# Cross attention and a two-way max MLP on one core: weight pieces of two row tiles by 512 columns, and a new order of the prologue

## The chip, the core and the metric

The kernel runs on one core of a Trainium2 chip. A core has five engines with a queue of instructions each: TensorE (PE in the profile, its weight loads PEld), VectorE (DVE), ScalarE (ACT), GpSimd (POOL) and SyncE (SP), which here only issues DMA transfers. Each engine works through its own queue in order and waits on semaphores for the others. Matrix products end in eight banks of PSUM, from which ACT and DVE copy them to SBUF; POOL does not read PSUM in this kernel. The metric is the device time of one execution, in microseconds (us).

## The reference

For each of 8 batches and 8 heads, x (512 x 64) and state (32 x 64) attend to each other; the results stand side by side in the 512 channels, and an MLP with the maximum of two projections follows.

```python
scores = scale * np.matmul(x, state.transpose(0, 1, 3, 2))
a = softmax(scores)                       # over the 32 states
xread = np.matmul(a, state)
scores2 = scale * np.matmul(state, x.transpose(0, 1, 3, 2))
a2 = softmax(scores2)                     # over the 512 positions
sread = np.matmul(a2, x)
# heads side by side: (8 * 544, 512)
h1 = x @ w1                               # 512 x 1024
h2 = x @ w2
g = np.maximum(h1, h2)
return (g @ w_out).astype(np.float32)     # 1024 x 512
```

(softmax stands for the four lines that subtract the maximum, take the exponential and divide by the sum.) Inputs and output are 32-bit floats.

## The kernel before, in words

The maximum is rewritten as max(h1 - h2, 0) + h2. So the kernel needs Wd = W1 - W2 (tile `wd`, line 429), W2 times W_out (tile `wwo`, built by TensorE from the transposed W2, tile `w2t`, line 437), and W_out itself in bf16 (tile `wo`). For a batch b it multiplies the state by Wd and by W2 W_out first (`sw_mm`, line 312, tile `sw`), so that the layer-1 product of the 512 positions is the attention weights times `sw` (`l1_mm`, line 345, followed by a ReLU into `r`), and layer 2 is `r` times W_out (`l2_f`, line 363) plus the attention weights times the last part of `sw` (`l2_open`, line 358).

Around that, for each batch: x is cast to bf16 in two layouts (`cast_e`, `cast_b`), transposed (`xt_mm` on TensorE for batches 0 and 1, `xt_dma` by a transposing DMA for the others), multiplied by the transposed state `sbd` for the scores (`sc_mm`, line 225), put through the exponential (`sc_ev`, line 243, ACT), summed (`red`, line 247, DVE) and scaled (`nmul`, line 251), and the weights are transposed (`at_mm` on TensorE for batch 0, `at_dma` on SP for the others).

The prologue takes in all weights and batches 0, 1 and part of 2. Its order is written out by hand in the string `ORDER` (lines 18 to 40), which `step` (line 522) reads token by token. A token with `>V`, `>A` or `>P` is a step on DVE, ACT or POOL; one with `:n` is a step of TensorE into bank n; one with neither is a DMA issued on SP. Each engine takes its own tokens in this order.

- `ldS.0.1`, `ldS.2.8`: the state of batch 0 and of batches 2 to 7; batch 1's is issued on ACT ahead of the list.
- `ldxk.0.k`: two heads of x of batch 0 (256 KB). `ldx.b.g`: four heads (512 KB).
- `ldw1.lo.hi`, `ldw2.lo.hi`: all 512 rows of W1 or W2, columns lo to hi (512 KB, 256 columns each, so runs of 1 KB). `ldwo.f0.f1`: 256 rows of W_out (512 KB, runs of 2 KB).
- `ce.b.k`, `xt.b.k`, `sc.b.h`, `red`, `nm`, `at.b.g`: cast, transpose, scores, sums, scaling, transposed weights.
- `cw2.q`, `w2.q`: cast and transpose of the qth piece of W2. `sub.q...`: Wd of that piece. `cwo.q`: cast of a quarter of W_out.
- `ww.i.f0.f1`: row tile i of W2 W_out, summed over the column tiles f0 to f1 of W2.
- `sw.b.z`: state times a 256-column quarter z of Wd (z below 4) or times W2 W_out (z = 4). `swh.b.z`: state times a 512-column half of Wd (z = 0, 1) or times W2 W_out (z = 2).
- `l1.b.f`: column tile f of layer 1. `l2p.b.c.f0.f1`: position tile c of layer 2, summed over f0 to f1. `l2o.b.c`: its part from the attention weights. `l2.b.c`: a whole one.
- `cSm.z`: the masked cast of the state of batches 2 to 7. `std`: its transposing DMA. `atd`, `xtd`: the two others. `store`: an output.
- `idle.n.w:i`: n matmuls of zeros, w columns wide (line 444), which leave bank i with nothing of use.

Behind the list stands a loop over the batches (line 540) and an end for the last one; in it TensorE does the layers of one batch and the scores and `sw` of the next.

## Time and profile before

| | us |
|---|---|
| median of 3 runs (150.14 to 150.85) | 150.24 |
| the profiled execution | 150.17 |
| its span in the trace | 148.4 |
| TensorE matmul busy | 140.4 |
| DVE busy | 81.5 |
| ACT busy | 69.0 |
| POOL busy | 48.9 |

Times in the trace count from the span's start. In an answer by order of time the first two columns are start and duration in us, then engine, line, operation, output and inputs, how often, and in brackets the idle time ahead of it and what ended it. Rows of neighbouring instructions of one kind are merged, so their duration is the stretch from the first to the end of the last. In a row of groups, the numbers behind the first bar are the sum in us and the mean in ns. The row of a DMA issue ends with its size and the us from issue to landing. The digits of the page's rows are busy tenths in 40 equal slices of the span. A row of stretches gives the stretch, its length, the busy time of PE, PEld, DVE, ACT and POOL, the granted clock of TensorE, the DMA engines' busy share and GB/s; the granted clock is 1.00 in all of them.

### The profile page before, as it was taken

The numbers are of one execution on the slowest core, as the hardware profiler recorded it, in microseconds if no ns is written. First come the engines' busy times: TensorE is split into PE (matmuls) and PEld (weight loads), VectorE is DVE, ScalarE is ACT, GpSimd is POOL, SyncE is SP. The second block draws the span as 40 slices with busy tenths as digits, with TensorE's granted clock in tenths as the row PEclk, the third lists the DMA queues.
The fourth block names the chain that finished last, engine by engine and source line by source line (L and its number), as shares of the span: only waits on it lengthen the run. The fifth ranks groups of instructions, "written<-read, shape, count | busy, mean of one in ns | idle before, by whom it ended". The sixth has DMA issues, their size and how long they took to land. (4 is left out here: it accounts for less than half of the span.)

```text
span 148.4 us, 3137 instructions
## 1 busy us (share of the span) xinstructions
PE 140.4 (95%) x1252; PEld 70.6 (48%) x1271; DVE 81.5 (55%) x161; ACT 69.0 (47%) x132; POOL 48.9 (33%) x74
## 2 busy tenths in 40 slices
PE   6879999999999999999999999999999999999991
...
DMA  4899999974998899499599577867306032400523
GB/s 116 276 371 364 361 351 361 267 228 81 213 283 309 148 272 364 87 148 331 222 170 272 236 196 129 274 286 141 75 0 283 0 75 106 179 9 9 200 82 141
DMA packets 39283, 29.74 MB, mean 200 GB/s; under 512 B 24160, under 2 KB 36704, under 8 KB 38368
## 3 DMA queue, kind: packets, MB, share of 16 engines
...
q8 instruction: 11, 0.18, 0.5%
q10 hardware_dynamic: 272, 0.07, 0.2%
q14 instruction: 8, 0.07, 0.2%
...
## 5 line engine op out<-in xcount | busy, mean ns | idle before, releaser
L365 PE MATMUL bank<-wo,r 128*128 128x512 bf16 (+1 forms) x260 | 60.6, 372 | 0.9 <-issue 0.3
L365 PEld LDWEIGHTS <-r 128*128 128x128 bf16 x264 | 25.5, 98 | 29.2 <-issue 1.0
L94 ACT COPY h<-bank 128x512 f32<-128x512 f32 (+1 forms) x15 | 8.6, 571 | 49.7 <-PE bank L365 49.7
L350 PE MATMUL bank<-aT,sw 128*128 128x512 bf16 x127 | 29.9, 379 | 0.1
L341 DVE TENSOR_SCALAR r<-bank 128x512 bf16<-128x512 f32 x28 | 19.4, 691 | 19.1 <-PE bank L350 18.6
L252 POOL TENSOR_TENSOR a<-e,er 128x512 bf16<-128x512 bf16 x16 | 17.1, 1084 | 34.1 <-DVE er L249 20.2
L339 ACT ACTIVATE r<-bank 128x512 bf16<-128x512 f32 x36 | 21.3, 611 | 7.6 <-PE bank L350 7.2
L96 DVE CAST sw<-bank 128x512 bf16<-128x512 f32 (+1 forms) x25 | 14.8, 643 | 14.2 <-PE bank L320 14.2
L98 POOL CAST xb<-h 128x1024 bf16<-128x1024 f32 x12 | 12.1, 1040 | 23.1 <-DMA h<-in_x_dram 12.4
L350 PEld LDWEIGHTS <-sw 128*128 128x128 bf16 x128 | 12.2, 98 | 13.6 <-ACT sw L94 0.2
L96 DVE COPY h<-bank 128x512 f32<-128x512 f32 (+1 forms) x18 | 11.7, 660 | 11.0 <-PE bank L365 10.2
L98 POOL CAST xe<-h 128x512 bf16<-128x512 f32 x27 | 15.7, 622 | 4.3 <-DMA h<-in_x_dram 2.6
L360 PE MATMUL bank<-sw,aT 128*128 128x512 bf16 (+1 forms) x54 | 16.5, 372 | 0.3
L94 ACT CAST sw<-bank 128x512 bf16<-128x512 f32 (+1 forms) x27 | 13.5, 569 | 3.0 <-PE bank L320 2.9
L248 DVE TENSOR_REDUCE sums<-e 128x16 f32<-128x512 bf16 x16 | 10.6, 662 | 1.0 <-ACT e L244 1.0
L444 PE MATMUL bank<-wz 128*128 128x256 bf16 (+1 forms) x48 | 8.9, 321 | 1.2 <-DVE ones L449 1.2
L244 ACT ACTIVATE e<-bank 128x512 bf16<-128x512 f32 x16 | 8.9, 595 | 1.4 <-PE bank L236 0.9
L360 PEld LDWEIGHTS <-aT 128*128 128x128 bf16 x66 | 5.6, 98 | 5.1 <-issue 0.5
L437 PE MATMUL bank<-wo,w2t 128*128 128x512 bf16 x31 | 7.9, 380 | 0.1
L444 PEld LDWEIGHTS <-wz 128*128 128x128 bf16 x48 | 4.8, 109 | 2.6 <-DVE ones L449 1.2
L320 PE MATMUL bank<-wd,sbd 64*32 64x512 bf16 (+1 forms) x144 | 5.6, 359 | 0.3 <-DVE wd L429 0.3
L429 DVE TENSOR_TENSOR wd<-h,h 128x512 bf16<-128x512 f32 x7 | 5.8, 862 | 0.1
...
## 6 DMA issues: line engine op xcount, KB each, us to landing
...
h<-in_moe_w_dram SPq DMA_DIRECT2D x8, 512.0 KB, 9.6
h<-in_moe_w_out_dram SPq DMA_DIRECT2D x4, 512.0 KB, 9.6
h<-in_x_dram SPq DMA_DIRECT2D x4, 512.0 KB, 9.8
...
```

The source lines that it names most:

```text
L94: nc.scalar.copy(o, i)
L96: nc.vector.tensor_copy(o, i)
L98: nc.gpsimd.tensor_copy(o, i)
L244: nc.scalar.activation(out=e_view(b, hh).rearrange("p (g c) i n -> p g c (i n)", g=2), in_=p.rearrange("p (c g m) -> p g c m", c=NC, g=2), ...
L248: nc.vector.tensor_reduce(es_all[:, b, hh], e_view(b, hh), axis=AXX, op=ALU.add)
L252: (nc.gpsimd if eng == "P" else nc.vector).tensor_mul(e_view(b, hh, "a"), e_view(b, hh), d_(b)["er"][:, hh].unsqueeze(3).to_broadcast([128 ...
L339: nc.scalar.activation(out=o, in_=p, func=ACTF.Relu)
L341: nc.vector.tensor_scalar(o, p, scalar1=0.0, scalar2=None, op0=ALU.max)
L350: nc.tensor.matmul(p, SW[b][:, g, f * 128:(f + 1) * 128], AT[b][:, g].rearrange("p c t -> p (c t)"), start=(g == 0), stop=(g == 1))
L360: nc.tensor.matmul(p[:, lo:hi], AT[b][:, g, c, :], SW[b][:, g, FF + lo:FF + hi], start=(start and g == 0), stop=(stop and g == 1))
L365: nc.tensor.matmul(p[:, lo:hi], R[b][:, f, c * 128:(c + 1) * 128], wo[:, f, lo:hi], start=(start and j == 0), stop=(stop and j == len(fs) ...
L444: nc.tensor.matmul(banks[i][:, 0:w], wz[:, 0:128], wz[:, 0:w], start=True, stop=True)
```

## The change

The pieces of W1 and W2 become two row tiles (256 rows) by 512 columns, still 512 KB, now with runs of 2 KB. A piece q has the column half q // 2 and the row tiles q % 2 * 2 and the next. Its cast, transposes, eviction and differences follow: a difference is now one row tile by 512 columns (`sub.q.k`), where it was two row tiles by 256. x of batch 0 comes in two loads of four heads. The state of batch 2 is transposed by TensorE (`S.2.3`, `S2`), so that the transposing DMA has batches 3 to 7. x of batch 3 comes in two loads. Batch 0 uses `swh` for both halves of Wd where it used four `sw`. The order of the prologue is new, and with it the engine of many casts, evictions and scalings and the number of filler matmuls.

```diff
 ORDER = """
-ldS.0.1 ldxk.0.0 ldxk.0.1 ldxk.0.2 ldxk.0.3 ldw2.0.256 ldwo.0.2 ldw1.0.256 ldw2.256.512 ldwo.2.4 ldw1.256.512
-ldw2.512.768 ldwo.4.6 ldw1.512.768 ldx.1.0 ldx.1.1 ldw2.768.1024 ldwo.6.8 ldw1.768.1024 ldS.2.8 ldx.2.0 ldx.2.1
-idle.4.512:7 cS.0.1>V S.0.1:0 cS.1.2>A idle.1.256:2 S.0.1.0>V S.0.1.1>V S.1.2:1 idle.5.256:6 S.1.2.0>A S.1.2.1>A
-ce.0.0>V xt.0.0:2 idle.6.256:7 xt.0.0>A ce.0.1>A ce.0.2>A xt.0.1:6 idle.1.256:5 ce.0.3>V xt.0.1>A xt.0.2:7 xt.0.3:5
-xt.0.2>A sc.0.0:3 xt.0.3>V sc.0.0>A sc.0.1:4 idle.6.256:1 cw2.0>V sc.0.1>A red.0.0>V w2.0:0 idle.10.256:2 w2.0>A
-cwo.0>V red.0.1>V nm.0.0>P ww.1.0.2:1 ww.2.0.2:2 sub.0.2.4>V ww.3.0.2:6 ww.0.0.2:7 sub.0.0.2>V idle.4.256:4 cw2.1>A
-nm.0.1>P sw.0.0:5,3 idle.5.256:0 sw.0.0.1>V sw.0.0.0>V w2.1:4 cwo.1>V at.0.0:0 w2.1>A at.0.1:3 idle.6.256:5
-at.0.0>V at.0.1>A ww.1.2.4:1 sub.1.0.2>V ww.3.2.4:6 sub.1.2.4>V l1.0.0:5 l1.0.1:0 l1.0.0>V sw.0.1:4,3 l1.0.1>A
-ww.0.2.4:7 cw2.2>V ww.2.2.4:2 sw.0.1.1>A sw.0.1.0>A swh.1.0:5,0 w2.2:3 swh.1.0.1>A l2p.0.0.0.2:4 cwo.2>P w2.2>V
...
+ldS.0.1 ldx.0.1 ldx.0.0 ldw2.1 ldwo.0.2 ldw2.0 ldw1.0 ldw1.1 ldwo.2.4 ldx.1.1 ldw2.3 ldw2.2 ldwo.4.6 ldwo.6.8
+ldw1.2 ldw1.3 ldx.1.0 ldx.2.1 ldx.2.0 ldS.2.8 idle.4.512:7 cS.0.1>V S.0.1:6 cS.1.2>P idle.1.256:2 S.0.1.0>A
+S.0.1.1>A S.1.2:7 idle.8.256:3 S.1.2.0>A S.1.2.1>V ce.0.3>V ce.0.2>A xt.0.3:2 xt.0.2:3 xt.0.3>V idle.4.256:5
+xt.0.2>V ce.0.1>A ce.0.0>V sc.0.1:4 xt.0.1:5 sc.0.1>A xt.0.0:0 xt.0.1>V idle.6.256:6 cw2.1>A xt.0.0>V red.0.1>V
+sc.0.0:1 sc.0.0>A w2.1:6 cwo.0>P idle.10.256:2 red.0.0>V w2.1>A nm.0.1>P ww.2.0.2:7 cw2.0>A ww.3.0.2:2 nm.0.0>V
+idle.3.256:4 w2.0:3 sub.0.1>V at.0.1:4 w2.0>A at.0.0:5 idle.6.256:1 sub.0.0>V sub.1.0>V at.0.0>A ww.0.0.2:0
+ww.1.0.2:1 at.0.1>A sub.1.1>V idle.3.256:5 cwo.1>V swh.0.0:6,3 swh.1.0:5,4 swh.0.0.1>A swh.0.0.0>V ww.0.2.4:0
+swh.1.0.0>A ww.1.2.4:1 ce.1.3>V l1.0.0:3 swh.1.0.1>A ww.3.2.4:2 l1.0.0>V ce.1.2>A ww.2.2.4:7 xt.1.3:6 l1.0.1:5
+xt.1.3>A xt.1.2:4 l1.0.3:3 l1.0.1>A cw2.3>P xt.1.2>V l1.0.2:6 l1.0.3>A sc.1.1:4 l1.0.2>V l2p.0.0.0.2:5 sc.1.1>A
+cw2.2>P w2.3:3 l2p.0.0.2.4:5 red.1.1>V w2.3>A l2p.0.2.0.2:6 l2p.0.2.2.4:6 nm.1.1>V cwo.2>A w2.2:4 l2p.0.3.0.2:3
+w2.2>V l2p.0.3.2.4:3 cwo.3>P ww.3.4.6:2 ww.0.4.6:0 ww.2.4.6:7 sub.2.1>V ww.0.6.8:0 sub.2.0>V ww.3.6.8:2 ww.0>A
+ww.2.6.8:7 sub.3.1>V ww.3>A ww.1.4.6:1 ww.1.6.8:1 sub.3.0>V ww.2>A l2p.0.1.0.2:4 ww.1>A ce.1.1>V swh.0.1:0,2
+ce.1.0>P l2p.0.1.2.4:4 swh.0.1.1>A swh.0.1.0>V xt.1.1:7 xt.1.0:1 xt.1.1>V l1.0.5:2 xt.1.0>A cb.2.1>P l1.0.4:0
+l1.0.5>A l1.0.7:7 l1.0.4>V ce.2.2>P sc.1.0:1 l1.0.6:2 sc.1.0>A l1.0.7>V ce.2.1>P l2p.0.1.4.6:4 l1.0.6>A
+l2p.0.0.4.6:5 red.1.0>V cb.2.0>P swh.1.2:0,1 sw.0.4:7,2 cSm.1>A l2p.0.2.4.6:6 nm.1.0>V l2p.0.2.6.8:6 swh.1.2.0>A
+ce.2.3>P sw.0.4.1>V l2p.0.3.4.6:3 atd.1 cSm.0>A l2p.0.1.6.8:4 ce.2.0>P swh.1.1:0,2 l2p.0.0.6.8:5 sw.0.4.0>A
+swh.1.1.1>V xtd.2 std ldx.3.0 ldx.3.1 l2p.0.3.6.8:3 swh.1.2.1>A swh.1.1.0>V l2o.0.2:6 l2o.0.0:5 l2.0.2>A S.2.3:7
+l2o.0.1:4 S2>V l2.0.0>A l1.1.6:2 l2.0.1>A l1.1.4:1 l1.1.3:0 l1.1.6>A l1.1.4>V l1.1.2:6 l1.1.1:7 l1.1.3>V l1.1.2>A
+l1.1.0:5 l1.1.1>V l1.1.5:4 l1.1.0>A l1.1.7:2 l1.1.5>V sc.2.0:1 l1.1.7>A l2o.0.3:3 sc.2.1:0 sc.2.0>A l2.1.0:6
+l2.0.3>A store.0 red.2.0>V sc.2.1>A nm.2.0>P red.2.1>V l2.1.1:7 l2.1.0>V nm.2.1>P atd.2 l2.1.1>A
 """
...
-    def load_w(w, src, lo, hi):
-        h, o = lo // 512, lo // 512 * 512
-        nc.sync.dma_start(out=half(w, h)[:, :, lo - o:hi - o], in_=src[:, lo:hi].rearrange("(i p) f -> p i f", p=128))
+    def load_w(w, src, q):
+        h, i = q // 2, q % 2 * 2
+        nc.sync.dma_start(out=half(w, h)[:, i:i + 2, :],
+                          in_=src[128 * i:128 * i + 256, 512 * h:512 * h + 512].rearrange("(i p) f -> p i f", p=128))
...
-        nc.sync.dma_start_transpose(out=sbd[:, 2:B].rearrange("p b (g k) t -> p (b g) (k t)", g=2),
-                                    in_=sb[:, 2:B].rearrange("p b g z d -> p (b g z d)"))
+        nc.sync.dma_start_transpose(out=sbd[:, 3:B].rearrange("p b (g k) t -> p (b g) (k t)", g=2),
+                                    in_=sb[:, 3:B].rearrange("p b g z d -> p (b g z d)"))
...
+    def s_ev2(p, eng):
+        copy(eng, sbd[:, 2].rearrange("p k t -> p (k t)"), p[:, 0:256])
...
-        w2b[q] = stage.tile([128, 4, FQ], BF16, tag="w2b", bufs=2, name="w2b")
-        copy(eng, w2b[q], half(2, q // 2)[:, :, q % 2 * FQ:q % 2 * FQ + FQ])
+        w2b[q] = stage.tile([128, 2, 512], BF16, tag="w2b", bufs=2, name="w2b")
+        copy(eng, w2b[q], half(2, q // 2)[:, q % 2 * 2:q % 2 * 2 + 2, :])
...
-        for f in range(2):
-            for i in range(4):
-                nc.tensor.transpose(p[:, (f * 4 + i) * 128:(f * 4 + i + 1) * 128],
+        for f in range(4):
+            for i in range(2):
+                nc.tensor.transpose(p[:, (f * 2 + i) * 128:(f * 2 + i + 1) * 128],
...
-        copy(eng, w2t[:, 2 * q:2 * q + 2].rearrange("p f i t -> p (f i t)"), p)
+        h, i = q // 2 * 4, q % 2 * 2
+        copy(eng, w2t[:, h:h + 4, i:i + 2], p.rearrange("p (f i t) -> p f i t", f=4, i=2))
...
-    def w_sub(q, i0, i1, eng):
-        c = slice(q % 2 * FQ, q % 2 * FQ + FQ)
+    def w_sub(q, k, eng):
+        h, i = q // 2, q % 2 * 2 + k
         (nc.gpsimd if eng == "P" else nc.vector).tensor_sub(
-            wd[:, i0:i1, q * FQ:(q + 1) * FQ], half(1, q // 2)[:, i0:i1, c], half(2, q // 2)[:, i0:i1, c])
+            wd[:, i, h * 512:(h + 1) * 512], half(1, h)[:, i, :], half(2, h)[:, i, :])
...
         if b + 3 < B:
-            load_x(b + 3, 0, 8)
+            for g in range(2 if b == 1 else 1):
+                load_x(b + 3, g, 4 if b == 1 else 8)
```

The rest of the old order, in the same notation (the lines left out above):

```
swh.1.0.0>A l1.0.3:0 l1.0.2:5 l1.0.3>A ww.3.4.6:6 sub.2.2.4>V l1.0.2>A ww.0.4.6:7 ww.2.4.6:2 sub.2.0.2>V ww.1.4.6:1
ce.1.0>V sw.0.2:3,0 l2p.0.0.2.4:4 sw.0.2.1>A sw.0.2.0>V ce.1.1>P xt.1.0:5 l1.0.4:0 xt.1.0>V xt.1.1:3 ce.1.2>P
l1.0.4>A l1.0.5:5 xt.1.1>V ce.1.3>P xt.1.2:0 l1.0.5>A sc.1.0:3 xt.1.2>V sc.1.0>A xt.1.3:5 cw2.3>V l2p.0.0.4.6:4
xt.1.3>A l2p.0.3.0.2:0 red.1.0>V w2.3:3 sc.1.1:5 cwo.3>A w2.3>V l2p.0.3.2.4:0 nm.1.0>P l2p.0.3.4.6:0 sc.1.1>A
ww.1.6.8:1 sub.3.2.4>V ww.0.6.8:7 ww.1>A ww.2.6.8:2 sub.3.0.2>P ww.0>V l2p.0.2.0.2:3 ww.2>A l2p.0.2.2.4:3 red.1.1>V
cSm.1>A l2p.0.2.4.6:3 sw.0.3:5,1 nm.1.1>P swh.1.1:7,2 sw.0.3.1>V sw.0.3.0>A ww.3.6.8:6 cSm.0>A swh.1.1.0>V l1.0.7:5
cb.2.0>P atd.1 l1.0.6:1 swh.1.1.1>V ww.3>A l2p.0.1.0.2:7 l1.0.6>V l2p.0.1.2.4:7 cb.2.1>P l1.0.7>A l2p.0.1.4.6:7
sw.0.4:2,6 ce.2.2>P xtd.2 swh.1.2:1,5 sw.0.4.0>A l2p.0.1.6.8:7 swh.1.2.0>V ce.2.3>P l2p.0.2.6.8:3 swh.1.2.1>A
l2p.0.3.6.8:0 ce.2.0>P sw.0.4.1>A l1.1.4:2 ce.2.1>P l1.1.0:1 l1.1.4>A l1.1.3:5 l1.1.0>A l2o.0.2:3 l1.1.3>V l1.1.6:6
l1.1.1:2 l2.0.2>V l1.1.6>A l1.1.2:1 std ldx.3.0.8 l1.1.1>A l2o.0.1:7 l1.1.2>V l1.1.5:5 l1.1.7:3 l2.0.1>V l1.1.5>A
l2p.0.0.6.8:4 l1.1.7>A l2o.0.0:4 l2o.0.3:0 l2.0.0>V sc.2.0:2 sc.2.1:1 l2.0.3>V store.0 sc.2.0>A sc.2.1>A l2.1.0:6
red.2.0>V red.2.1>V nm.2.0>P nm.2.1>P l2.1.0>A l2.1.1:7 l2.1.1>A atd.2
```

17 lines of the change are left out of this document (3 added, 14 removed).

## The prediction

> **What bounds the kernel now.** I read the first page, then TensorE's order of time over the prologue, then the loads.
>
> ```profile
> span 148.4 us, 3137 instructions
> PE 140.4 (95%) x1252; PEld 70.6 (48%) x1271; DVE 81.5 (55%) x161; ACT 69.0 (47%) x132; POOL 48.9 (33%) x74
> PE   6879999999999999999999999999999999999991
> DMA  4899999974998899499599577867306032400523
> ```
>
> TensorE is busy 95% of the span, and its row drops below 9 only in the first slices and the last. But a busy TensorE at the start is partly filler: line 444 multiplies zeros to bridge waits. So I count useful work.
>
> ```profile
> 10.97 1.25 PE L444 MATMUL bank<-wz 128*128 128x256 bf16 x10
> 12.24 1.90 PE L437 MATMUL bank<-wo,w2t 128*128 128x512 bf16 x7
> 17.38 1.04 PE L437 MATMUL bank<-wo,w2t 128*128 128x512 bf16 x4
> 18.25 1.03 PE L350 MATMUL bank<-aT,sw 128*128 128x512 bf16 x3
> 48.05 0.63 PE L320 MATMUL bank<-wd,sbd 64*32 64x512 bf16 x16
> ```
>
> The first layer-1 step of batch 0 (l1.0.0, L350) starts at 18.25; the prologue's list of steps is through at 48.05, where the loop's first L320 starts. From there on nothing is edited but the size of two transfers, so I take every us by which 48.05 moves as a us at the end. The question is when l1.0.0 can start, what TensorE must do behind it, and whether it is fed.
>
> Unit prices, from differences of starts:
>
> ```profile
> 54.01 3.62 PE L350 MATMUL bank<-aT,sw 128*128 128x512 bf16 x16
> 57.46 0.63 PE L236 MATMUL bank<-sbd,xt 128*128 128x64 bf16 x16
> 15.66 0.61 PE L420 MATMUL bank<-ident,w2b 128*128 128x128 bf16 x8
> 16.11 0.61 PE L274 MATMUL bank<-ident,a 128*128 128x128 bf16 x8
> 43.18 0.63 PE L236 MATMUL bank<-sbd,xt 128*128 128x64 bf16 x16
> 43.64 0.59 PE L360 MATMUL bank<-sw,aT 128*128 128x512 bf16 x2
> 19.21 0.30 PE L320 MATMUL bank<-wd,sbd 64*32 64x256 bf16 x8
> 19.44 1.04 PE L437 MATMUL bank<-wo,w2t 128*128 128x512 bf16 x4
> 20.41 0.41 PE L320 MATMUL bank<-wd,sbd 64*32 64x512 bf16 x8
> 20.75 0.62 PE L420 MATMUL bank<-ident,w2b 128*128 128x128 bf16 x8
> ```
>
> Sixteen 512-column matmuls take 57.46 - 54.01 = 3.45, so 0.2155 each and 0.431 a pair (each l1, each two-step ww or l2p, each l2o is a pair). Eight transposes take 0.45 (16.11 - 15.66), so an xt (four) 0.225 and a w2 0.45. An sc is half of 43.64 - 43.18, 0.23. A quarter sw step: L350's four matmuls from 18.25 end at 19.11, and L437 starts at 19.44, so 0.33. A half step (swh): L437's four end at 20.30, next start 20.75, so 0.45. A quarter has 0.11 of streaming and a half 0.215, so each switch to these small tiles costs about 0.22 beside the streaming.
>
> Now the loads. They wait in one queue, and those who wait for them date the landings:
>
> ```profile
> 9.77 0.69 DVE L96 CAST w2b<-h 128x1024 bf16<-128x1024 f32 x1 [1.15 <-DMA h<-in_moe_w_dram]
> 14.13 1.04 ACT L94 CAST w2b<-h 128x1024 bf16<-128x1024 f32 x1 [1.95 <-DMA h<-in_moe_w_dram]
> 23.66 0.43 DVE L96 CAST xe<-h 128x512 bf16<-128x512 f32 x1 [0.21 <-DMA h<-in_x_dram]
> 7.09 1.55 SPq L148 DMA_DIRECT2D h<-in_moe_w_dram  x1
> h<-in_moe_w_dram SPq DMA_DIRECT2D x1, 512.0 KB, 9.9
> 28.08 1.17 SPq L141 DMA_DIRECT2D h<-in_x_dram  x1
> h<-in_x_dram SPq DMA_DIRECT2D x1, 512.0 KB, 5.6
> ```
>
> Of the 512 KB pieces behind x0, the 1st lands at 9.77, the 4th at 14.13, the 6th (issued 7.09, 9.9 to landing) at 16.99, the 10th at 23.66, the last load of all at 28.08 + 5.6 = 33.7. That is 7.22 / 5 = 1.44 a piece early and 13.89 / 9 = 1.54 over the nine.
>
> ```profile
> 2.50:3.00 0.50, 0.50 (x2) 0.00 (x0) 0.10 (x1) 0.24 (x2) 0.00 (x0) 1.00 0.57 180
> 6.00:6.50 0.50, 0.45 (x5) 0.16 (x2) 0.00 (x0) 0.50 (x2) 0.00 (x0) 1.00 0.86 184
> 8.50:9.00 0.50, 0.42 (x9) 0.41 (x10) 0.12 (x1) 0.50 (x2) 0.00 (x0) 1.00 1.06 377
> 20.00:20.50 0.50, 0.50 (x11) 0.09 (x8) 0.18 (x1) 0.45 (x2) 0.00 (x0) 1.00 1.09 350
> 28.00:28.50 0.50, 0.50 (x7) 0.26 (x4) 0.50 (x2) 0.50 (x2) 0.00 (x0) 1.00 0.87 160
> ```
>
> The last two columns are DMA share and GB/s. The queue runs full at 350 to 377 from about 8 us, but is below that in two early places: 180 at 2.5 us, while x0's four loads are issued one after the other, and 184 at 6 us, where the first 1 KB runs of W2 follow x0.
>
> **The change, part by part.** Two DMA issues fewer for x0, and the first W2 piece in 2 KB runs. Both bear on the two dips. If nothing comes of it, the first piece lands at 9.77 as before. If both dips filled to 370, 0.5 us at 180 and 0.5 us at 184 would each give back some 0.25 us, and their neighbours about as much again: 8.8. I take 9.3, the middle, since the first dip has a cause that the change removes and the second only a suspected one.
>
> Pace behind it: the early rows' 1.44 a piece mixes 1 KB runs of W with 2 KB runs of W_out. If run length is nothing, 1.44 stays; if W went at the 377 shown at 8.5 us instead of the 350 at 20 us, a piece gains 0.1. I take 0.05 for each W piece.
>
> By the Trainium skill ("DMA: Bandwidth & Descriptors", Specifications) a transfer is at line rate from runs of 512 B up, so 1 KB and 2 KB runs should go alike. By that rule the 0.05 would be nothing, 0.15 us on the sum; the windows agree so far, as 350 and 377 differ by 8% at most.
>
> The new order needs W1 and W2 in whole column halves, all four row tiles, before swh.0.0, where the old one needed a quarter for sw.0.0. So w1.1, the 5th piece, and W_out's second quarter (ldwo.2.4), the 6th, set l1.0.0. The 6th lands at 9.3 + 7.22 - 3 x 0.05 = 16.37. Then DVE, in its order, casts it (cwo.1), TensorE does ww.0.2.4 and ww.1.2.4, and l1.0.0 follows. Durations:
>
> ```profile
> L96 DVE CAST wo<-h 128x1024 bf16<-128x1024 f32 x2 | 1.3, 657 | 0.0
> 17.10 1.29 DVE L429 TENSOR_TENSOR wd<-h,h 128x512 bf16<-128x512 f32 x2
> 12.68 2.14 DVE L429 TENSOR_TENSOR wd<-h,h 128x512 bf16<-128x512 f32 x2
> 11.50 2.78 POOL L252 TENSOR_TENSOR a<-e,er 128x512 bf16<-128x512 bf16 x2 [9.05 <-DVE er L249]
> L168 ACT ACTIVATE sb<-sf,zm 128x768 bf16<-128x768 f32 x2 | 1.9, 938 | 0.0
> L94 ACT CAST sw<-bank 128x512 bf16<-128x512 f32 x23 | 12.1, 602 | 1.5 <-PE bank L320 1.5
> sf<-in_state_dram SPq DMA_DIRECT2D x1, 384.0 KB, 9.1
> aT<-a SPq DMA_TRANSPOSE x7, 3.2
> ```
>
> 16.37 + 0.66 + 0.06 + 0.86 = **17.95** for l1.0.0. The other way in is covered: w1.1 lands about 14.95, two subs (0.645 each, row at 17.10) end at 16.25, swh.0.0 with swh.1.0 beside it takes 0.45 + 0.215 = 0.67 to 16.9, before cwo.1's 17.03; its eviction on DVE behind cwo.1 ends near 17.8, under the two ww pairs.
>
> Behind l1.0.0 TensorE has the same ww, l1, l2p, l2o, l2, w2, xt and sc as before. What differs: before, five groups of small tiles are left (0.33 + 0.45 + 0.33 + 0.56 + 0.65 = 2.32: sw.0.1, swh.1.0, sw.0.2, then sw.0.3 with swh.1.1, then sw.0.4 with swh.1.2); now three (0.45 + 0.65 + 0.45 = 1.55). S.2.3, batch 2's state on TensorE, adds two transposes, 0.11. Before, l1.0.0 to 48.05 took 29.80; now 29.80 - 0.77 + 0.11 = 29.14, if it stalls as much as it did. 17.95 + 29.14 = 47.09, **0.96 earlier**. Break-even is l1.0.0 at 18.91.
>
> Fillers (41 small ones for 44) only bridge waits that the loads set; they cost nothing while the load is later, and 0.11 each if it isn't. The moves of casts and evictions between ACT, DVE and POOL lie under TensorE, with DVE and ACT about half busy, except at two places.
>
> First, S.2.8 goes to the end of the queue, and ACT holds its mask (cSm.1) ahead of swh.1.2.0, cSm.0 and sw.0.4.0. Behind them wait swh.1.1, which needs the bank that swh.1.2.0 empties, and l2o.0.2, which needs sw.0.4.0. From l1.0.0 to swh.1.1 lie 32 pairs (13.8), 4 xt (0.9), 2 sc (0.46), 2 w2 (0.9), and two groups of small tiles (1.1): 17.15, so 35.1; l2o.0.2 follows 0.45 + 0.86 later, at 36.4. ACT needs 0.94 + 0.60 + 0.94 + 0.60 + 0.1 = 3.2 from S's landing, so S may land at 33.2. When will it? x2.0 is the 16th piece: 16.37 + 10 x 1.55 - 4 x 0.05 = 31.7. S's 384 KB take 1.1 us at 350 GB/s or 2.5 at the 160 shown at 28 us, where S's short runs pass: 32.8 to 34.2. I take the middle, 33.4 to 33.5: a wait of some **0.2**.
>
> Second, batch 1's nmul moves from POOL to DVE. No row shows it on DVE. Bounds: 0.645, the sub alone, and 1.07, the sub beside POOL work (row at 12.68). From sc.1.0 at about 31.4: exponential and latency 0.8, reduction and reciprocal 0.95, nmul 0.65 to 1.07, transposing DMA 3.2: 37.0 to 37.4; l1.1.6, which needs it, comes at 37.7. No cost, with 0.3 to 0.7 to spare.
>
> The SP queue: atd.1, xtd.2 and std wait behind S's issue, as before behind x2's. xtd.2 is due at sc.2.0 near 41, atd.1 issues at about 34, xtd.2 behind it near 35.7 as in the old run, so it is hidden; std now carries five batches and is due one loop turn later. x3 in two loads adds one issue with 10 us to spare.
>
> Sum: 0.96 - 0.2 = 0.8 of the profiled run's 150.17 (span 148.4 and 1.77 around it): 149.37. The runs' median is 0.07 above the profiled one, so **149.4**.
>
> **Rivals.**
> (A) As forecast, l1.0.0 between 17.4 and 18.2: 148.6 to 149.6.
> (B) The loads come no earlier: first piece at 9.77, 6th at 16.99, l1.0.0 at 18.57, gain 0.34: 149.9. For it: the queue is full from 8 us on in both run lengths. Against: the two dips.
> (C) S too late. It passes alone at the end of the queue, in short runs behind x2. Every 0.1 us past 33.2 is 0.1 us at l2o.0.2. From 34.2 the gain is eaten; a landing at 35.0 gives 150.24 - 0.96 + 1.8 = 151.1. For it: ACT is blocked in order, and 160 GB/s at 28 us. Against: the old run, with S in the middle, had its last load in by 33.7, and the bytes are the same.
> (D) nmul on DVE beside POOL's casts. POOL has five casts of x2 just when nm.1.0 runs; in the old run the sub took 1.07 instead of 0.645 beside POOL, and POOL's multiply (two in 2.78) suffered too. If nm.1.0 waited for a whole 1.04 us cast and DVE's subs took 1.07 at swh.0.0, l1.0.0 loses 0.4 and l1.1.6 about 0.5: gain near 0, 150.2. Against: POOL is idle at the subs.
> The Trainium skill has a rule for (D) ("SBUF — State Buffer", Who interferes with whom): a DVE instruction with two SBUF inputs contends with POOL instructions that read SBUF, and the loser waits the whole instruction. The two sub rows agree; by it nm.1.0 would pay up to a full cast.
>
> **How the numbers follow.** About 0.75 us (0.5%) is what a measurement here tells from no change. A 0.45, B 0.22, C 0.21, D 0.12. Faster: A but for its last 0.1 us or so (0.43) and a little of B (0.02), 0.45. Slower: C with S landing at about 35 (0.17), and D with S's wait on top of it (0.05), 0.22. Same: the rest, 0.33, most of it B. A's own range is 148.6 to 149.6; for 8 in 10 the range goes up to 150.9, nearly to C's end.
>
> **What would show it.** Right: first w2b cast (on ACT) near 9.3 and l1.0.0 near 18.0; the loop's first L320 near 47.3; ACT idle before cSm.1 for sf near 33.4. Wrong: l1.0.0 past 18.9; TensorE idle at swh.0.1 or xt.1.0 for late loads (w1.3, x1.0); TensorE idle before L360 or the second layer-1 run. A later difference in the loop would break the premise that the end moves with 48.05.

## The result and the profile after

The changed kernel took 148.51 us (median of 6 runs, 148.14 to 148.71) against 150.19 for the kernel before (6 runs, 149.72 to 150.85): a ratio of 0.9883, with a 95% interval of 0.9857 to 0.9909. The gain is 1.68 us, a little over twice the 0.8 forecast, and the time lies 0.09 under the low end of the range. The profiled execution took 148.61.

The first page of the changed kernel, same rows as before:

```profile
span 146.8 us, 3122 instructions
PE 140.1 (95%) x1254; PEld 69.8 (48%) x1254; DVE 82.2 (56%) x160; ACT 70.5 (48%) x132; POOL 46.5 (32%) x72
PE   6599999999999999999999999999999999999991
DMA  4999999942999987995779686777406032400524
```

The span is 1.6 us shorter and TensorE's busy time 0.3: most of what went is idle time of TensorE. The order of time shows where. Line numbers are those of the changed kernel: L353 is layer 1, L323 `sw`, L441 `ww`, L433 the differences, L255 the scaling, L168 the masked cast of the state, L222 the transposes of x, L448 the filler.

```profile
9.13 1.05 ACT L93 CAST w2b<-h 128x1024 bf16<-128x1024 f32 x1
11.80 1.32 DVE L255 TENSOR_TENSOR a<-e,er 128x512 bf16<-128x512 bf16 x1
13.26 2.59 DVE L433 TENSOR_TENSOR wd<-h,h 128x512 bf16<-128x512 f32 x4
15.93 0.69 DVE L95 CAST wo<-h 128x1024 bf16<-128x1024 f32 x1
16.73 0.69 DVE L95 CAST sw<-bank 128x512 bf16<-128x512 f32 x1
17.60 0.59 PE L353 MATMUL bank<-aT,sw 128*128 128x512 bf16 x2
32.97 0.94 ACT L168 ACTIVATE sb<-sf,zm 128x768 bf16<-128x768 f32 x1 [0.28 <-DMA sf<-in_state_dram]
46.55 0.63 PE L323 MATMUL bank<-wd,sbd 64*32 64x512 bf16 x16
```

Layer 1 of batch 0 (l1.0.0) starts at 17.60 (18.25 before) and the loop at 46.55 (48.05 before). So 0.65 us come ahead of l1.0.0, and 0.85 between it and the loop, 28.95 for 29.80. From the loop's start to the span's end it is 100.25 now and 100.35 before: the 1.50 us reach the end whole.

The loads of the changed kernel, by the rows of its issues; the queue's start times come first, then what a window around single issues says (size, us to landing), for x0's two halves, W2's first piece, W_out's second quarter and the late state S (issued at 23.73):

```profile
1.26 1.00 SPq L140 DMA_DIRECT2D h<-in_x_dram  x2
2.31 0.51 SPq L147 DMA_DIRECT2D h<-in_moe_w_dram  x1
5.76 0.54 SPq L152 DMA_DIRECT2D h<-in_moe_w_out_dram  x1
```

```profile
h<-in_x_dram SPq DMA_DIRECT2D x1, 512.0 KB, 5.1
h<-in_x_dram SPq DMA_DIRECT2D x1, 512.0 KB, 6.0
h<-in_moe_w_dram SPq DMA_DIRECT2D x1, 512.0 KB, 6.8
h<-in_moe_w_out_dram SPq DMA_DIRECT2D x1, 512.0 KB, 10.2
sf<-in_state_dram SPq DMA_DIRECT2D x1, 384.0 KB, 9.2
```

The first piece lands at 2.31 + 6.8 = 9.11 and the sixth at 5.76 + 10.2 = 15.96, so (15.96 - 9.11) / 5 = 1.37 a piece where it was 1.44. And the stretches of the changed kernel (last two columns: DMA share and GB/s):

```profile
8.00:10.00 2.00, 1.84 (x30) 1.52 (x30) 1.53 (x5) 1.81 (x3) 0.00 (x0) 1.00 1.03 392
10.00:12.00 2.00, 1.88 (x24) 1.40 (x21) 1.64 (x5) 1.87 (x4) 1.48 (x2) 1.00 1.05 402
24.50:28.50 4.00, 4.00 (x20) 1.66 (x17) 2.70 (x5) 1.82 (x4) 0.95 (x1) 1.00 1.09 352
31.50:32.50 1.00, 1.00 (x8) 0.39 (x4) 0.99 (x3) 0.91 (x2) 1.00 (x3) 1.00 0.07 17
```

With runs of 2 KB the queue moves 392 to 402 GB/s; where x (runs of 1 KB) passes, 352. The last row comes back below. At the prediction's two dips the changed kernel has

```profile
2.50:3.00 0.50, 0.50 (x2) 0.00 (x0) 0.00 (x1) 0.24 (x2) 0.00 (x0) 1.00 0.57 76
6.00:6.50 0.50, 0.00 (x0) 0.00 (x0) 0.07 (x1) 0.07 (x1) 0.00 (x0) 1.00 0.99 309
```

The first dip is deeper (76 for 180 GB/s). The second is gone (309 for 184), but 209 stands at 7.5 us, where the kernel before has 350. From 2 to 8 us both kernels move the same, 274 GB/s before and 273 now. So the dips did not fill, and yet the first piece came earlier: its issue moved from 3.29 to 2.31 us, and it landed 6.8 us behind it, where it took 6.5 before.

### The profile page after: what moved, and what is told of

It reads as the page before. It is cut to its first block, busy times and chain, and to the rows that moved or that the text cites. A ratio compares the mean times of both kernels' runs of the same rounds, so it can differ in the third digit from the quotient of the medians.

```text
span 146.8 us, 3122 instructions
## 1 busy us (share of the span) xinstructions
PE 140.1 (95%) x1254; PEld 69.8 (48%) x1254; DVE 82.2 (56%) x160; ACT 70.5 (48%) x132; POOL 46.5 (32%) x72
## 5 line engine op out<-in xcount | busy, mean ns | idle before, releaser
L368 PE MATMUL bank<-wo,r 128*128 128x512 bf16 (+1 forms) x264 | 61.5, 373 | 0.1
L93 ACT COPY h<-bank 128x512 f32<-128x512 f32 (+1 forms) x18 | 10.1, 575 | 50.9 <-PE bank L368 50.0
L344 DVE TENSOR_SCALAR r<-bank 128x512 bf16<-128x512 f32 x32 | 21.9, 690 | 18.9 <-PE bank L353 17.9
L353 PE MATMUL bank<-aT,sw 128*128 128x512 bf16 x128 | 29.6, 380 | 0.0
L342 ACT ACTIVATE r<-bank 128x512 bf16<-128x512 f32 x32 | 19.4, 614 | 4.3 <-PE bank L353 4.0
L95 DVE CAST sw<-bank 128x512 bf16<-128x512 f32 x23 | 14.7, 684 | 11.8 <-PE bank L323 11.6
L255 POOL TENSOR_TENSOR a<-e,er 128x512 bf16<-128x512 bf16 x13 | 13.4, 1048 | 24.4 <-ACT e L247 14.9
L363 PE MATMUL bank<-sw,aT 128*128 128x512 bf16 (+1 forms) x66 | 19.1, 374 | 0.0
L353 PEld LDWEIGHTS <-sw 128*128 128x128 bf16 x128 | 12.0, 98 | 13.2 <-DVE sw L95 0.2
L95 DVE COPY h<-bank 128x512 f32<-128x512 f32 (+1 forms) x15 | 9.8, 660 | 10.2 <-PE bank L368 10.2
L93 ACT CAST sw<-bank 128x512 bf16<-128x512 f32 x25 | 13.2, 600 | 1.2 <-PE bank L323 1.2
L448 PE MATMUL bank<-wz 128*128 128x256 bf16 (+1 forms) x45 | 8.1, 316 | 1.2 <-DVE ones L453 1.2
L441 PE MATMUL bank<-wo,w2t 128*128 128x512 bf16 x32 | 7.8, 380 | 0.0
L239 PEld LDWEIGHTS <-xt 128*128 128x128 bf16 x128 | 5.1, 98 | 2.9 <-DVE xt L95 0.9
L433 DVE TENSOR_TENSOR wd<-h,h 128x512 bf16<-128x512 f32 x8 | 5.2, 688 | 1.3 <-DMA h<-in_moe_w_dram 1.2
L448 PEld LDWEIGHTS <-wz 128*128 128x128 bf16 x45 | 4.5, 107 | 2.7 <-DVE ones L453 1.2
```

What stands on the lines that cost most here:

```text
L93: nc.scalar.copy(o, i)
L95: nc.vector.tensor_copy(o, i)
L255: (nc.gpsimd if eng == "P" else nc.vector).tensor_mul(e_view(b, hh, "a"), e_view(b, hh), d_(b)["er"][:, hh].unsqueeze(3).to_broadcast([128 ...
L342: nc.scalar.activation(out=o, in_=p, func=ACTF.Relu)
L344: nc.vector.tensor_scalar(o, p, scalar1=0.0, scalar2=None, op0=ALU.max)
L353: nc.tensor.matmul(p, SW[b][:, g, f * 128:(f + 1) * 128], AT[b][:, g].rearrange("p c t -> p (c t)"), start=(g == 0), stop=(g == 1))
```

## The experiments

All are edits of the changed kernel unless the text says "old order". Ratios are to the kernel before, with the 95% interval.

**1. Is it the run length? w_runs_1k** loads each W piece by two transfers of 256 columns, so that runs are 1 KB again; **w_rows_1** loads it by two transfers as well, but of one row tile each, with runs of 2 KB.

In `load_w`, w_runs_1k:

```diff
+        for c in range(2):
+            nc.sync.dma_start(out=half(w, h)[:, i:i + 2, 256 * c:256 * c + 256],
+                              in_=src[128 * i:128 * i + 256, 512 * h + 256 * c:512 * h + 256 * c + 256].rearrange("(i p) f -> p i f", p=128))
```

and w_rows_1:

```diff
+        for c in range(2):
+            nc.sync.dma_start(out=half(w, h)[:, i + 1 - c, :],
+                              in_=src[128 * (i + 1 - c):128 * (i + 1 - c) + 128, 512 * h:512 * h + 512])
```

> The changed kernel, but each piece of W1 and W2 is loaded by two transfers of 256 columns (256 KB each, runs of 1 KB). Theory (the longer runs set the pace of the load queue, and the 6th piece behind x0 sets l1.0.0): the 6th piece lands at 16.4 to 17.0 instead of 15.96, l1.0.0 starts at 18.0 to 18.6 instead of 17.60, and the time is 149.0 to 149.5. Rival (run length is nothing, the gain is the order's): GB/s between 9 and 14 us as in the changed kernel (390 to 410), time 148.3 to 148.7.

> The changed kernel, but each piece of W1 and W2 is loaded by two transfers of one row tile (256 KB each, runs of 2 KB as in the changed kernel): the control for the number of transfers. Both theories: 148.2 to 148.8, l1.0.0 within 0.3 of 17.60. If more transfers cost something by themselves, it is slower here too, and what the 1 KB version loses beyond this one is the run length's.

Measured: w_runs_1k 149.35 us, 0.9928 (0.9909 to 0.9946); w_rows_1 148.42, 0.9872 (0.9851 to 0.9892). Both have twice as many transfers, and only the one with short runs loses: 0.93 us between the two, with intervals that don't meet. So the number of transfers costs nothing here, and the run length is worth some 0.8 us, about half the gain. The profile of w_runs_1k is of its longest execution (150.18), so I take the price from the medians. But the mechanism is in it: 351 GB/s from 12 to 14 us, l1.0.0 at 18.52 (theory: 18.0 to 18.6; w_rows_1 has 17.19), and behind it TensorE waits 0.50 us for x of batch 1, at 20.48.

**2. What a run costs. stream** only loads, piece behind piece, first all of W1 and W2 in 1 KB runs, then 2 KB, then 4 KB, and then x, W_out, and W1 and W2 again.

> Loads alone, nothing computed and only the first 128 rows of the output written (with zeros): in this order 4 MB of W1 and W2 in runs of 1 KB (all rows by 256 columns), 4 MB in runs of 2 KB (two row tiles by 512 columns), 4 MB in runs of 4 KB (one row tile by all columns), 4 MB of x in runs of 1 KB that follow each other in memory, 2 MB of W_out in runs of 2 KB, then 2 KB and 1 KB runs of W again. Theory (run length sets the pace of a full queue): 345 to 365 GB/s in both stretches of 1 KB runs and in x, 385 to 410 with 2 KB, at least that with 4 KB. Rival (the bank layout of W or what runs beside it sets it): no difference between 1 KB and 2 KB beyond 2%, or x unlike W.

```profile
8.00:14.00 6.00, 0.00 (x0) 0.00 (x0) 1.00 1.10 353
20.00:24.00 4.00, 0.00 (x0) 0.00 (x0) 1.00 1.05 386
26.00:32.00 6.00, 0.00 (x0) 0.00 (x0) 1.00 1.03 411
```

(Here the columns are stretch, length, DVE, POOL, granted clock, DMA share, GB/s.) In this one execution it is 353 GB/s at 1 KB, 386 at 2 KB, 411 at 4 KB: a piece of 524,288 bytes takes 1.485, 1.358 and 1.276 us. The first step saves 0.127 us for 256 runs fewer, the second 0.082 for 128 fewer: 0.50 and 0.64 ns a run over sixteen engines, so 8 to 10 ns of one engine for each run. Neither the tensor nor the place in the stream matters: x in 1 KB runs goes at 349 from 38 to 44 us, W_out in 2 KB runs at 386 to 388 from 52 to 56, and W1 and W2 later, in the reverse order, at 387 (56 to 60) and 348 to 349 (66 to 76). That leaves nothing for the rival, the layout of W. The price also dates the kernels: before, three W pieces and two of W_out between the first and sixth landing make 3 x 1.485 + 2 x 1.358 = 7.17 (7.22 in the trace); now 5 x 1.358 = 6.79 (6.85).

The Trainium skill ("DMA: Bandwidth & Descriptors", Specifications) puts line rate at 512 B and up; 353 against 386 and 411 contradict it. A section of the same page, "Why small descriptors are slow (HBM only)", names a fixed overhead per packet, which is roughly the form the three rates have.

**3. x0 in two loads: x0_four** goes back to four loads (heads 4 to 7 first, as the new order wants them); **old_x0_two** puts two loads into the old order; **x0_one** has one load of 1 MB.

```diff
-ldS.0.1 ldx.0.1 ldx.0.0 ldw2.1
+ldS.0.1 ldxk.0.2 ldxk.0.3 ldxk.0.0 ldxk.0.1 ldw2.1
...
-ldS.0.1 ldxk.0.0 ldxk.0.1 ldxk.0.2 ldxk.0.3 ldw2.0.256
+ldS.0.1 ldx.0.0 ldx.0.1 ldw2.0.256
...
-ldS.0.1 ldx.0.1 ldx.0.0 ldw2.1
+ldS.0.1 ldx.0.0.8 ldw2.1
```

> The changed kernel, with x of batch 0 in four loads of two heads (heads 4 to 7 first). Theory (the queue is what is full, so two issues more cost nothing): the first piece of W2 lands within 0.2 of 9.11, time 148.3 to 148.7. Rival (the early dips came from the four issues, as the prediction took it): the first piece lands 0.4 to 0.6 later and the time is 148.9 to 149.2.

> The kernel before, with x of batch 0 in two loads of four heads and nothing else changed. Theory (at the start the landing of the first W2 piece follows its issue, 6.2 to 7.0 us behind it in every trace so far, so two x loads less bring every piece about 1 us forward): the first piece lands near 8.8 to 9.2 instead of 9.79, l1.0.0 starts 0.6 to 1.0 earlier than 18.25, time 0.6 to 1.2 less than the kernel before. Rival (what x0_four lost belongs to the new order, which waits for heads 4 to 7 in another way): within 0.3 of the kernel before.

> The changed kernel, with x of batch 0 in one load of 1 MB. Theory (landing follows issue): W2's first piece is issued 0.5 earlier and lands near 8.6; x0 lands as a whole near 7.2 to 7.7, so its eight transposes come later but still before W2's: time 147.9 to 148.4. Rival (bytes decide, and the four heads that came first were worth something): 148.5 to 149.0.

Measured: x0_four 150.06, 0.9982 (0.9964 to 1.0000). old_x0_two 151.01, 1.0025 (0.9999 to 1.0051). x0_one 150.48, 1.0008 (0.9986 to 1.0031). From x0_four:

```profile
1.26 1.98 SPq L140 DMA_DIRECT2D h<-in_x_dram  x4
3.29 0.47 SPq L147 DMA_DIRECT2D h<-in_moe_w_dram  x1
10.32 1.04 ACT L93 CAST w2b<-h 128x1024 bf16<-128x1024 f32 x1 [1.30 <-DMA h<-in_moe_w_dram]
18.79 0.59 PE L353 MATMUL bank<-aT,sw 128*128 128x512 bf16 x2
```

Two issues more put W2's issue from 2.31 to 3.29, and its cast from 9.13 to 10.32, where ACT waits for the load. l1.0.0 is 1.19 late and most of the gain is gone. (The profiled execution takes 150.18, 1.57 over the changed kernel's: 1.23 at the loop's start, and 0.37 behind it, where the granted clock reads 0.96 from 140 us on.) So within the new order, x0's two loads carry most of it. One load is no better: x0_one issues W2's piece 0.56 earlier, at 1.75, but it lands 7.5 us later, at 9.25, and x0 as a whole at 7.36, so both its theory (an earlier piece) and its rival fell. But in the old order they bring nothing, although W2's first piece is issued at 2.30 there too:

```profile
8.93 1.03 PE L219 MATMUL bank<-ident,xe 128*128 128x128 bf16 x8
10.34 0.68 DVE L96 CAST w2b<-h 128x1024 bf16<-128x1024 f32 x1
```

The piece lands 6.9 us behind its issue, at 9.2, and is cast at 10.34: DVE works in order, and the cast stands behind the last copy of x0's transposes. It did not wait for the load (no bracket), and l1.0.0 comes at 19.52. My theory (0.6 to 1.2 us faster) fell: the load was early and its reader wasn't. Note also the eight transposes in 1.03 us instead of 0.62; experiment 7 and the last section come back to it.

**4. Batch 2's state: std_six** transposes it by DMA again.

```diff
-swh.1.1.1>V xtd.2 std ldx.3.0 ldx.3.1 l2p.0.3.6.8:3 swh.1.2.1>A swh.1.1.0>V l2o.0.2:6 l2o.0.0:5 l2.0.2>A S.2.3:7
-l2o.0.1:4 S2>V l2.0.0>A
+swh.1.1.1>V xtd.2 std ldx.3.0 ldx.3.1 l2p.0.3.6.8:3 swh.1.2.1>A swh.1.1.0>V l2o.0.2:6 l2o.0.0:5 l2.0.2>A
+l2o.0.1:4 l2.0.0>A
...
-        nc.sync.dma_start_transpose(out=sbd[:, 3:B].rearrange("p b (g k) t -> p (b g) (k t)", g=2),
-                                    in_=sb[:, 3:B].rearrange("p b g z d -> p (b g z d)"))
+        nc.sync.dma_start_transpose(out=sbd[:, 2:B].rearrange("p b (g k) t -> p (b g) (k t)", g=2),
+                                    in_=sb[:, 2:B].rearrange("p b g z d -> p (b g z d)"))
```

> The changed kernel, with the state of batch 2 transposed by the DMA again (six batches in one transfer, no S.2.3 and S2). Theory (it stands behind xtd.2 on SP, issued near 37.8 with some 5 us to landing): sc.2.0 waits until about 43.2 instead of 41.2, the loop starts about 1.8 later, time 150.0 to 150.5. Rival (the wait was covered anyway, as in the old kernel): the same or 0.1 faster, 148.3 to 148.6.

Measured: 149.02, 0.9920 (0.9893 to 0.9947), some 0.5 us over the changed kernel, where I expected 1.5 to 2; the two intervals overlap a little.

```profile
41.18 0.39 PE L239 MATMUL bank<-sbd,xt 128*128 128x64 bf16 x8 [0.50 <-DMA sbd<-sb]
```

The scores of batch 2 wait for the transposing DMA. The last matmul ahead of them starts at 40.30 and needs 0.22, so they are 0.66 late (0.50 in the bracket, which counts from the modelled end of that matmul). Less the 0.11 of the two transposes, that is 0.55, as the ratios have it. The wait is real, but TensorE's two transposes buy half a us, no more. (The profile is of the shortest of six executions.)

**5. S late: s_late** puts half of batch 3's x ahead of S in the queue (512 KB, some 1.4 us).

```diff
-ldx.2.0 ldS.2.8
+ldx.2.0 ldx.3.0 ldS.2.8
```

> The changed kernel, with the first half of x of batch 3 (512 KB) loaded ahead of the state of batches 2 to 7, whose landing so moves from 32.9 to about 34.4. The prediction's rival C: ACT's mask waits, swh.1.1 or l2o.0.2 waits behind it, 0.1 us for each 0.1 us past 33.2 (33.0 with the earlier l1.0.0): the loop starts 1.0 to 1.4 later, time 149.5 to 150.0. Rival theory (there is more room than was counted): the same time as the changed kernel, 148.3 to 148.8.

```profile
34.26 0.93 ACT L168 ACTIVATE sb<-sf,zm 128x768 bf16<-128x768 f32 x1 [1.78 <-DMA sf<-in_state_dram]
35.72 0.41 PE L323 MATMUL bank<-wd,sbd 64*32 64x512 bf16 x8 [0.68 <-ACT sw L93]
```

Measured: 148.94, 0.9898 (0.9863 to 0.9933). The mask comes 1.29 us later, the half step behind it waits for the bank that ACT frees (0.68 in the bracket, 0.75 by the starts), and the stretch from l1.0.0 to the loop grows by 0.91, to 29.86. The median grows by 0.4, by ratio by 0.15%, which is inside the intervals, so the profile shows the wait and the time does not. It is rival C's mechanism at the place it named. But of the 1.29 us only some 0.75 became a wait of TensorE; the rest was room that the changed kernel had left.

**6. Ways to start earlier. s_on_act** issues both first states in one load on ACT, which takes one issue from SP; **x0_on_act** issues x0's second half on ACT; **nm00_pool** puts batch 0's first scaling back on POOL; **both_moves** has the last two.

```diff
-        (nc.scalar if lo == 1 else nc.sync).dma_start(out=sf[:, lo:hi].rearrange("p b g d -> p (b g) d"),
+        (nc.scalar if lo < 2 else nc.sync).dma_start(out=sf[:, lo:hi].rearrange("p b g d -> p (b g) d"),
-    load_s(1, 2)
+    load_s(0, 2)
```

is s_on_act (its list begins with x0), and x0_on_act and nm00_pool are

```diff
-ldS.0.1 ldx.0.1 ldx.0.0 ldw2.1
+ldS.0.1 ldx.0.1 ldw2.1
+    xf_t[0] = h8(H, NC * D)
+    nc.scalar.dma_start(out=xf_t[0][:, 0:4, :], in_=x[0, 0:4].rearrange("h (p c) d -> p h (c d)", c=NC))
...
-nm.0.0>V
+nm.0.0>P
```

> The changed kernel, with the state of batches 0 and 1 in one load issued on ACT, so that SP issues x0 first. Theory (landing follows issue): all SP issues come about 0.5 earlier, the first W2 piece lands near 8.6, l1.0.0 at 17.0 to 17.2, time 147.9 to 148.2. Rival (the queue is full by then and bytes decide): as the changed kernel, 148.4 to 148.7.

> The changed kernel, with the second half of x of batch 0 issued on ACT, so that SP issues W2's first piece 0.5 earlier. Theory (its landing follows its issue, and x0 isn't later): the piece lands near 8.5, the first W2 cast starts near 8.6, l1.0.0 near 17.1, time 147.9 to 148.3. Rival (both halves of x0 share the engines, heads 4 to 7 land later, and the cast waits behind x0's work on ACT): cast near 9.5, time 148.7 to 149.2.

> The changed kernel, with the first scaling of batch 0 (nm.0.0) on POOL instead of DVE, where it took 1.32 us beside POOL's nm.0.1. Theory (in every run of the new order l1.0.0 starts 8.5 to 8.8 us behind the first W2 cast, through ACT, then DVE's reduction, scaling and four differences: DVE's queue binds as much as the loads): the differences start when w1.0 lands, not behind the scaling; l1.0.0 comes 8.2 to 8.5 behind the cast, time 148.2 to 148.5. Rival (the loads alone bind): 8.5 to 8.8 behind the cast, time 148.4 to 148.7.

> The changed kernel with nm.0.0 on POOL and the second half of x of batch 0 issued on ACT. Theory: the two chains, loads and DVE's queue, are shortened together: l1.0.0 near 16.8, time 147.6 to 148.2. Rival: 148.4 to 149.0.

Measured: s_on_act 150.12, 0.9969 (0.9944 to 0.9995); x0_on_act 149.88, 0.9952 (0.9916 to 0.9987); both_moves 150.24, 0.9978 (0.9949 to 1.0008): all slower than the changed kernel. nm00_pool 148.45, 0.9860 (0.9814 to 0.9905): the same as it. There the differences wait for W1 in place of the scaling:

```profile
13.41 2.68 DVE L433 TENSOR_TENSOR wd<-h,h 128x512 bf16<-128x512 f32 x4 [0.86 <-DMA h<-in_moe_w_dram]
```

so the 1.32 us that the scaling takes on DVE are covered by the load. In s_on_act the first W2 piece is issued at 1.79 and lands 6.5 later at 8.29, 0.8 earlier, but ACT, in its order, first waits for TensorE's scores and casts it at 10.86:

```profile
5.32 0.29 DVE L95 CAST sb<-sf 128x256 bf16<-128x256 f32 x1 [3.90 <-DMA sf<-in_state_dram]
10.37 0.60 ACT L247 ACTIVATE e<-bank 128x512 bf16<-128x512 f32 x1 [2.41 <-PE bank L239]
10.86 1.04 ACT L93 CAST w2b<-h 128x1024 bf16<-128x1024 f32 x1
```

The first row says why the scores are late: the first states, now in one load beside x0 and not ahead of it, land at 5.3 (their cast starts at 3.00 in the changed kernel), and ACT copies their transposes at 6.11 to 6.92, ahead of x0's casts. TensorE also ran at half speed there. So it did in the other two losers, as eight transposes of x0_on_act show (1.03 us, in the changed kernel 0.62), but also in nm00_pool's profiled execution (1.03 at 6.80), and that kernel is as fast as the changed one.

**7. Is the half-speed start the cause?** Filler matmuls ahead of x0, 14 in place of 8 (of 5 in the old order), on the changed kernel (**fill_after**), x0_on_act (**fill_x0_act**), both_moves (**fill_both**) and old_x0_two (**fill_old_x0**).

```diff
-idle.8.256:3
+idle.14.256:3
```

> The changed kernel with 14 filler matmuls instead of 8 ahead of the first transposes of x0. Theory (TensorE runs at half its speed until it has been busy long enough, and the changed kernel mostly gets there in time already): within 0.3 of the changed kernel, 148.2 to 148.7, transposes of x0 at 0.056 each. Rival (fillers cost their own time): each filler that runs past x0's landing delays the first transposes, 148.8 or more.

> The kernel of x0_on_act (second half of x0 issued on ACT), with 14 fillers instead of 8. In x0_on_act TensorE's first eight transposes of x0 took 1.03 instead of 0.62 and it stayed slow until about 10.9 us. Theory (the slow start is what made that kernel lose 1.4 us): with more fillers TensorE is fast by x0's landing, the first W2 cast starts 0.6 to 1.0 earlier than 10.04, time 148.3 to 148.9 instead of 149.88. Rival (loads on two queues are the cause): 149.6 to 150.2, TensorE fast or not.

> The kernel of both_moves (second half of x0 on ACT, nm.0.0 on POOL), with 14 fillers instead of 8. Theory: 148.0 to 148.8 instead of 150.24. Rival: 149.6 to 150.4.

> The kernel before with x0 in two loads (as old_x0_two, 151.01), with 14 fillers instead of 5 ahead of the first transposes. Theory (the old order with two x loads lost by the slow start, where TensorE stayed slow until about 11.9): 149.6 to 150.3. Rival (in the old order DVE's cast of W2 behind x0's eviction decides): 150.7 to 151.3.

| | without | with 14 fillers |
|---|---|---|
| changed kernel | 148.51, 0.9883 | 148.36, 0.9904 (0.9868 to 0.9939) |
| x0_on_act | 149.88, 0.9952 | 149.34, 0.9955 (0.9924 to 0.9987) |
| both_moves | 150.24, 0.9978 | 149.20, 0.9937 (0.9906 to 0.9967) |
| old_x0_two | 151.01, 1.0025 | 150.65, 1.0044 (1.0016 to 1.0071) |

The two columns come from different series of runs, so the ratios are to be compared. By them both_moves alone gains, with intervals that overlap a little; the others are unchanged. The mean granted clock of each execution fits that (a lower mean is a fall back to half speed after the start, as in the last section): in both_moves it was below 0.99 in 8 of 12 executions without the added fillers and in 1 of 12 with them. In old_x0_two it was below 0.99 in 7 of 12 (151.01 to 151.57 us); the other five took 149.35 to 150.98, no better than the kernel before. In all four profiles with 14 fillers the transposes run at full speed, as in fill_x0_act:

```profile
7.74 0.62 PE L222 MATMUL bank<-ident,xe 128*128 128x128 bf16 x8 [1.54 <-DVE xe L95]
10.26 1.05 ACT L93 CAST w2b<-h 128x1024 bf16<-128x1024 f32 x1 [0.23 <-DMA h<-in_moe_w_dram]
```

Yet none comes to the time of fill_after in the same series (148.36). The half-speed start was a part at most. With x0's halves issued on two engines, the halves land at 7.25 and 8.87 here, for 6.36 and 7.75 (1.26 + 5.1 and 1.75 + 6.0) in the changed kernel, and W2's first piece at 10.26 although it is issued 0.56 earlier, at 1.75. Single profiles scatter, though. Over the four profiles with a split issue the first cast of x0 starts at 6.15 to 7.25 and the first of the second half at 8.24 to 8.87; over the seven with both halves on SP it is 5.61 to 6.67 and 7.04 to 8.06. So the second half is late in all four, the first not in all. Why was not found. Nor was why the old order stays at the time before, or a little above it, with two loads of x0 and a TensorE at full speed (l1.0.0 at 18.11 in that profile, loop at 47.92): the first half of x0 is cast at 6.06 where the first quarter was at 4.71, and the five groups of small tiles are still there, but that it is these was not tried. No version beat the changed kernel beyond the intervals.

## Why the prediction was half right

The direction, the place and the chain (loads, then l1.0.0, then the loop's start, then the end) were right. Three steps failed: the size of the pace, the wait for S, which was put in and did not come, and the reason for the first piece, whose number came out right by luck.

**The pace behind the first piece: mis-sized.** I took 0.05 us for each W piece, from bounds of 0 and 0.1. It is 0.127 by the stream, above my upper bound. The bounds came from two stretches of half a us (377 and 350 GB/s), and I halved the difference because nothing in the profile of before kept the two kinds of run apart; stretches of one kind alone, 4 to 6 us long, give 386 and 353. With 0.127 and the three W pieces on the way the sixth lands 0.23 earlier than forecast.

**The first piece: 9.3 forecast, 9.11 in the trace.** The number is inside its bounds, but it was the middle between no dip filled and both filled, and by the rows above the queue moved no more by 8 us than before. What brought the piece forward is its earlier issue, from 3.29 to 2.31; x0_four, with 3.29 again, loses it. But an issue at 1.75 brought nothing more (x0_one: 9.25). And one profile does not fix the landing to 0.2: with W2 issued at 2.30 or 2.31 its first cast starts anywhere from 8.52 (std_six) to 9.64 (nm00_pool).

**l1.0.0: 17.95 forecast, 17.60 in the trace.** The sixth piece landed at 15.96 for 16.37, and 1.64 us lay behind it for 1.58. But by the rows above, DVE goes without a pause from the scaling at 11.80 to the copy of `sw` that ends at 17.42, and l1.0.0 follows. Load and DVE come out even in this execution, so I read from it that a faster load alone would not have brought more; nm00_pool shows the reverse, that a faster DVE doesn't either. Five more profiles of kernels with the same first loads have l1.0.0 at 17.14 to 18.14 (std_six and nm00_pool), so the 0.35 of this one is within their scatter.

**l1.0.0 to the loop: 29.14 + 0.2 forecast, 28.95 in the trace.** The 0.2 was a wait for S, with S at 33.4 to 33.5 and room to 33.2. S landed at 23.73 + 9.2 = 32.93, ACT waited 0.28 for it, and TensorE not at all. The room was mis-sized too: I added ACT's steps to 3.2 us from S to l2o.0.2, and in s_late, where TensorE waits for them, it is 2.76, from the mask at 34.26 to

```profile
37.02 1.02 PE L363 MATMUL bank<-sw,aT 128*128 128x512 bf16 x4
```

In the changed kernel l2o.0.2 starts at 36.39, so the room ended at 33.6: S at 33.5 would have cost nothing either.

The remaining 0.19 is stalls that I had let stand ("if it stalls as much as it did"). Between 18.25 and 48.05 they are here in the kernel before:

```profile
25.97 0.59 PE L350 MATMUL bank<-aT,sw 128*128 128x512 bf16 x2
26.51 0.38 PE L219 MATMUL bank<-ident,xe 128*128 128x128 bf16 x4
26.73 0.40 PE L236 MATMUL bank<-sbd,xt 128*128 128x64 bf16 x8
27.25 0.38 PE L219 MATMUL bank<-ident,xe 128*128 128x128 bf16 x4
25.86 1.34 ACT L339 ACTIVATE r<-bank 128x512 bf16<-128x512 f32 x2 [0.76 <-PE bank L350]
```

By the prices of the prediction (0.225 for an xt, 0.431 for a pair, 0.23 for an sc) the second row starts 0.11 late and the fourth 0.29; the first is 0.09 late, behind an xt at 25.66. The xt at 26.51 and 27.25 go into the banks of l1.0.4 and l1.0.5, which the two ACT steps of the last row empty, by about 26.5 and at 27.20. That makes 0.49. No bracket shows these waits, as a matmul's modelled end lies beyond the start of the next. In the changed kernel a stall of 0.22 and one of 0.06 (at 29.8) are left; the first waits for POOL's cast of W2:

```profile
20.87 0.60 PE L368 MATMUL bank<-wo,r 128*128 128x512 bf16 x2
21.52 0.45 PEld L423 LDWEIGHTS <-w2b 128*128 128x128 bf16 x8 [0.55 <-POOL w2b L97]
```

So the net is some 0.2. The prediction did not look for waits of this kind on either side. Seven other profiles of the new order lack the first of the two and take 28.72. Beware of the rows that look like stalls:

```profile
24.56 0.11 PEld L365 LDWEIGHTS <-r 128*128 128x128 bf16 x2
24.79 0.38 PE L365 MATMUL bank<-wo,r 128*128 128x512 bf16 x1 [0.16 <-issue]
```

Here l2p.0.0.2.4 is two matmuls, two weight loads are on record and one matmul is. The other falls into the idle time, which is a missing record.

**Together:** 0.35 at l1.0.0, 0.2 for S and 0.19 of stalls are 0.74, and 47.3 - 46.55 is 0.75. The profiled execution's 148.61 is 0.76 under the forecast 149.37. The runs' median lies 0.10 below it, where I had put it 0.07 above: without that difference the time would have stayed inside the range, if only just. The range's low end went with l1.0.0 at 17.4, which by itself is 149.4 - 0.55 = 148.85, so it left 0.25, about the wait for S, and nothing for stalls. Several small errors of one sign summed past it.

**Break-even at l1.0.0 = 18.91** is not contradicted: x0_four with 18.79 took 150.06, both_moves with 18.91 took 150.24 (ratios 0.9982 and 0.9978). The l1.0.0 are of one execution each, the times are medians.

**The rivals.** B (no earlier loads) is out: the first piece came 0.6 earlier. C is a true mechanism, with 0.4 us more room than counted, and wasn't reached. D's waits are real: the scaling on DVE took 1.32 us beside POOL's at 11.80, 1.15 beside its casts, and 0.69 with POOL idle but for the first 0.1 us,

```profile
33.23 1.15 DVE L255 TENSOR_TENSOR a<-e,er 128x512 bf16<-128x512 bf16 x1
22.71 0.69 DVE L255 TENSOR_TENSOR a<-e,er 128x512 bf16<-128x512 bf16 x1
```

but the first is covered by the load (nm00_pool), and behind the second (33.23) TensorE has no stall up to the loop. The rule of the Trainium skill ("SBUF — State Buffer", Who interferes with whom) is borne out by the rows and decides nothing.

**What was not in the sum at all:** what the transposes of batch 2's state save; I had only charged them (0.11). Without them the scores come 0.66 late (std_six). Before, the same scores came at 43.18 without a wait; it is the earlier order that needs them.

The parts don't add. By ratio, short runs cost 0.45% (0.9928 - 0.9883), four loads of x0 1.0%, the transposing DMA 0.37%, together 1.8% for a gain of 1.17%. That fits parts that are each on the path only while the others are in place; of the three, only x0's loads were tried in the old order as well.
